# A planned three-layer kernel on one core: the planner's durations set to those of a trace

## Chip, cores, metric

The kernel runs on one core of a Trainium2 chip, as one launch. The metric is device time in microseconds (us) of that launch; lower is better.

## What is computed

Three layers follow one another: local attention, a channel mix with a gate, and a token and channel mixer. Cut to what matters:

```
# attention: 4 batches x 8 heads, 576 positions, head size 64; each position sees 32 others
attn = softmax(mask(q @ k.T / 8)) @ v              # heads 0-3: the last 32; heads 4-7: every 4th of 128
x    = attn, heads side by side                    # (4, 576, 512)
# first mix
x_prev = x moved by one position
xk, xr = mu_k*x + (1-mu_k)*x_prev, mu_r*x + (1-mu_r)*x_prev
x    = sigmoid(xr @ w_r) * (relu(xk @ w_k)**2 @ w_v)      # w_k 512x1024, w_v 1024x512, w_r 512x512
# second mix
u    = x + (relu(x.T @ w_tok1) @ w_tok2).T
out  = u + relu(u @ w_ch1) @ w_ch2
```

The weights arrive as 64-bit floats and are turned into 32-bit ones on the chip.

## The kernel before

**The work.** Attention is cut into 36 units, nine for each batch (`attend`). A unit loads queries and keys (128x832 words, 416 KB) and values (96x512, 192 KB), makes scores on TensorE, a softmax on VectorE and ScalarE, transposes on TensorE, a copy out of PSUM, and then eight small 64x64 matmuls for each transpose group that weigh the values (`weigh`); the result goes to the buffers `xt`. The first nine units run alone; the other 27 are laid beside the first mix. Positions are taken in six chunks of 384. For each chunk `prep` mixes x with its predecessor (`z<-xt,cst`, one step into a scratch buffer, a second that adds), and splits the sum into a high half and a low half, because each fp32 product is made of three fp32r matmuls (`mm3`). `keys` multiplies the key operands with `w_k`, in the order of blocks `KT = [2, 3, 0, 1]` of the 512 channels; `receptance` multiplies with `w_r`; `mix` with `w_v`. For the first chunk the receptance operands are made by TensorE from `x` and diagonal matrices (`bank<-xt,wk`).

**Weights.** `weight` loads a piece into one of two raw buffers, and then takes five steps: ScalarE scales the upper words, VectorE does a shift (`TENSOR_SCALAR`), a bitwise merge and an add in 16-bit halves (two `SCALAR_TENSOR_TENSOR`), a copy gives the high half, and VectorE subtracts for the low half. The next but one piece can be loaded only when VectorE's third step has read the raw buffer. The pieces come in the order: w_k piece 1, w_r pieces 1 to 4, then w_v and w_k in turn.

**What sets the order.** The program is written into `Plan`, which records operations and their dependences. `order` walks a model of time: each engine takes, among the operations that are ready, the one that is due first; a due time is worked out backwards from the order of TensorE's operations in the program, with `_cost` as duration and `DELAY` as time from one engine to another. Copies and a few scalings may go to ScalarE or VectorE (`either`): the plan decides. The order of all five engines is then emitted as one fixed program; each engine keeps its row, in order, and waits on semaphores. All loads are issued by SyncE, in its own planned order. The model also holds a clock of TensorE (`_run`). Line 394 (396 after the change) is the `call(**kw)` that emits every operation, so all instructions carry it; they are told apart by tiles.

Of the kernel before, what the change touches and what calls it, by code (L numbers as in the profile page):

```python
# [64 lines left out]
class View:  # L65


    def __init__(self, slot, kind, array, dtype):
        self.slot, self.kind, self.array, self.dtype = slot, kind, array, dtype
# [76 lines left out]
class Plan:  # L146
# [16 lines left out]
        "sync": dict(tensor=1.09, vector=0.98, scalar=0.98, gpsimd=0.98, sync=1.4),  # L163
    }
    TICK, BUSY = 10.24 / 3, 3060

    def __init__(self, nc):
        self.nc = nc
# [68 lines left out]
    @staticmethod  # L237
    def _cost(engine, method, kw):

        out = kw["out"]  # L240
        cols = int(np.prod(out.shape[1:]))
        if engine == "sync":
            return max(0.45, 4 * cols * out.shape[0] / 310e3)
        if engine == "tensor":
            if method == "transpose":
                return cols / 1200 + 0.0025
            if kw["lhsT"].dtype in (F32R, BF16):
                return cols / 2400 + 0.0135
            if kw["lhsT"].shape[0] <= D or out.shape[0] <= D:
                return cols / 1200 + 0.0025  # L250
            return 2 * max(cols / 1200 + 0.0025, 0.112)
        source = kw.get("in_", kw.get("in0"))
        psum = source is not None and "PSUM" in str(source.space)
        if engine == "scalar":
            extra = sum(hasattr(kw.get(k), "space") for k in ("scale", "bias"))
            extra += 2 * (kw.get("accum_out") is not None)
            return (0.165 if psum else 0.215) + cols / 1200 + 0.093 * extra
        if engine == "gpsimd":
            return 0.04 if method == "memset" else 0.04 + cols / 345
        if method == "tensor_reduce":  # L260
            return 0.145 + int(np.prod(source.shape[1:])) / 960
        if method == "reciprocal":
            return 0.145 + cols / 157
        fast = method in ("tensor_copy", "tensor_scalar", "tensor_scalar_add") and not psum
        return 0.145 + cols / (1920 if fast else 960)

    def _run(self, at, cost, kw):

# [13 lines left out]
    def order(self):  # L282
        n = len(self.ops)
        after = [[] for _ in range(n)]
        for i, deps in enumerate(self.deps):
            for d in deps:
                after[d].append(i)
        first = [next(iter(op)) for op in self.ops]
        cost = [op[e][2] for op, e in zip(self.ops, first)]
        due, t = [1e9 + i for i in range(n)], 0.0  # L290
        for i, e in enumerate(first):
            if e == "tensor":
                due[i], t = t, t + cost[i]
        for i in reversed(range(n)):
            pad = 0 if first[i] == "tensor" else 1.0
            for s in after[i]:
                due[i] = min(due[i], due[s] - cost[i] - self.DELAY[first[i]][first[s]] - pad)
        for i, e in self.early.items():
            due[i] -= e
        for group in self.bursts:  # L300
            due[group[0]] = min(due[i] for i in group)
            for k, i in enumerate(group[1:]):
                due[i] = -1e6 + k
        left = [len(d) for d in self.deps]
        ready = [dict.fromkeys(op, 0.0) for op in self.ops]
        known = {e: [] for e in self.ENGINES}
        avail = {e: [] for e in self.ENGINES}
        free = dict.fromkeys(self.ENGINES, 0.6)
        free["sync"] = 1.7
        start, engine = [None] * n, [None] * n  # L310
        self.tick, self.columns, self.warm, late = 0, 0.0, False, 0.0

        def learn(i):
            for e in self.ops[i]:
                heapq.heappush(known[e], (ready[i][e], i))

        for i in range(n):
            if not left[i]:
                learn(i)
        for _ in range(n):  # L320
            best = None
            for e in self.ENGINES:
                for q in (avail[e], known[e]):
                    while q and start[q[0][1]] is not None:
                        heapq.heappop(q)
                if avail[e]:
                    at = free[e]
                elif known[e]:
                    at = max(free[e], known[e][0][0])
                else:  # L330
                    continue
                if best is None or at < best[0]:
                    best = at, e
            at, e = best
            while known[e] and known[e][0][0] <= at + 0.1:
                _, i = heapq.heappop(known[e])
                if start[i] is None:
                    heapq.heappush(avail[e], (due[i], i))
            aside, chosen = [], None
            while avail[e]:  # L340
                item = heapq.heappop(avail[e])
                i = item[1]
                if start[i] is not None:
                    continue
                ends = {}
                for o in self.ops[i]:
                    ahead = 0.0
                    if o != e:
                        ahead = 1.0 * sum(self.ops[j][o][2] for d, j in avail[o] if d < due[i] and start[j] is None)
                    ends[o] = max(max(at, free[o]) + ahead, ready[i][o]) + self.ops[i][o][2]  # L350
                pick = first[i]
                if ends[pick] > due[i] + cost[i] + late + 0.0:
                    pick = min(ends, key=ends.get)
                if pick == e:
                    chosen = item
                    break
                aside.append(item)
            if chosen is None:
                chosen = aside.pop(0)
            for item in aside:  # L360
                heapq.heappush(avail[e], item)
            i = chosen[1]
            at = max(at, ready[i][e])
            method, kw, length = self.ops[i][e]
            end = at + length
            if e == "tensor":
                end = self._run(at, length, kw)
                late = max(late, at - due[i] if due[i] >= 0 else 0.0)
            start[i], engine[i] = at, e
            free[e] = end  # L370
            for s in after[i]:
                for o in self.ops[s]:
                    ready[s][o] = max(ready[s][o], end + self.DELAY[e][o])
                left[s] -= 1
                if not left[s]:
                    learn(s)
        self.engine = engine
        return sorted(range(n), key=lambda i: (start[i], i))
# [672 lines left out]
```

## Time and profile before

| | |
|---|---|
| runs | 715.89, 716.20, 716.91 us; median 716.2 |
| profiled execution | span 715.3 us from first to last instruction; no time of its own is given beside it. The runs lie 0.6 to 1.6 us above that span |
| TensorE | busy 697.9 us (98%) |
| VectorE, ScalarE | busy 405.1 us (57%), 295.7 us (41%) |
| loads and stores | 53.84 MB, 75 GB/s over the span; about 300 GB/s in the first 30 us |
| TensorE without work | 12.3 us of the first 29.69 us, 1.4 us from there to 56.00 us, none to 711.66 us, 3.6 us at the end |

Since TensorE is busy for 98% of the span, the first 56 us are where its idle time lies.

### The profile page before, as it was taken

What the parts mean: (1) busy time and instruction counts of PE and PEld (TensorE: products, weight loads), DVE (VectorE), ACT (ScalarE), POOL (GpSimd) and SP (SyncE); (2) the same over time, 40 slices, a digit from 0 to 9 for tenths busy, and PEclk for the clock granted to TensorE, in tenths of its full rate; (3) what the DMA queues carried; (4) which work ended last, traced back from release to release, by engine and by line L of the source; (5) the groups of instructions that cost most, each with busy time, mean ns of one, the idle gap of its engine ahead of it and who ended that gap; (6) DMA issues with size and microseconds to landing.
All of it is one profiled execution on the core that took longest, in us unless ns stands there. A gap on an engine that the chain in (4) does not pass through costs nothing.

```text
span 715.3 us, 10559 instructions
## 1 busy us (share of the span) xinstructions
PE 697.9 (98%) x4090; PEld 599.5 (84%) x4090; DVE 405.1 (57%) x915; ACT 295.7 (41%) x825; POOL 2.2 (0%) x22
## 2 busy tenths in 40 slices
PE   6699999999999999999999999999999999999997
PEld 6568988888898888888889988888888888888897
DVE  5799987686586688675888998132123112211121
ACT  5688786565364463453676543121111111111110
POOL 0000000000000000000000000000000000000000
PEclk9799999999999999999999999999999999999999
DMA  8956722224222101103222252001001000100010
GB/s 298 282 203 220 254 76 78 71 89 132 61 71 71 36 9 41 41 15 114 86 74 89 89 175 61 1 0 60 0 1 60 0 1 0 60 1 0 1 60 30
DMA packets 26082, 53.84 MB, mean 75 GB/s; under 512 B 2480, under 2 KB 10032, under 8 KB 26032
## 3 DMA queue, kind: packets, MB, share of 16 engines
q1 hardware_dynamic: 26032, 53.17, 22.9%
q8 instruction: 32, 0.52, 0.3%
q14 instruction: 18, 0.15, 0.1%
HBM read 48.44 MB, written 4.72 MB: 74 GB/s over the span
## 4 chain that ended last, share of the span: by engine, by line
PE 93%; DMA 3%; DVE 1%; ACT 1%; SPq 0%; issue 0%; ACTq 0%
PE bank L394 93%; DMA x<-w_k 1%; DMA wv<-units 1%; DMA x<-w_r 1%; DVE x L394 1%; ACT x L394 1%; SPq L394 0%; DVE z L394 0%; ACT wv L394 0%; ACT z L394 0%; ACT at L394 0%; DVE wr L394 0%; DVE at L394 0%; DVE xt L394 0%; ACTq L394 0%
## 5 line engine op out<-in xcount | busy, mean ns | idle before, releaser
L394 PE MATMUL bank<-z,wk 128*128 128x384 f32 (+2 forms) x816 | 197.7, 357 | 0.5 <-DVE z L394 0.3
L394 DVE SCALAR_TENSOR_TENSOR z<-bank,z 128x512 fp32r<-128x512 f32 (+2 forms) x116 | 70.3, 606 | 218.5 <-ACT z L394 217.7
L394 ACT ACTIVATE z<-bank 128x512 fp32r<-128x512 f32 (+3 forms) x120 | 63.5, 529 | 278.7 <-PE bank L394 277.2
L394 PEld LDWEIGHTS bank<-z,wk 128*128 128x128 f32 x816 | 146.6, 188 | 15.6 <-DVE z L394 0.6
L394 PE MATMUL bank<-wv,z 128*128 128x512 f32 x432 | 125.8, 402 | 0.5 <-ACT wv L394 0.5
L394 PE MATMUL bank<-z,x 128*128 128x512 f32 (+1 forms) x540 | 120.2, 371 | 0.0
L394 PEld LDWEIGHTS bank<-z,x 128*128 128x128 f32 x540 | 94.9, 188 | 18.8
L394 PEld LDWEIGHTS bank<-wv,z 128*128 128x128 f32 x432 | 78.6, 188 | 14.1 <-ACT wv L394 0.6
L394 PE MATMUL bank<-z,at 128*128 128x512 f32 (+1 forms) x276 | 69.0, 383 | 0.0
L394 PE MATMUL bank<-wr,z 128*128 128x512 f32 x228 | 66.8, 404 | 0.0
L394 PEld LDWEIGHTS bank<-z,at 128*128 128x128 f32 x276 | 48.5, 188 | 8.6
L394 DVE TENSOR_TENSOR z<-z,z 128x384 fp32r<-128x384 f32 x92 | 49.9, 551 | 5.6 <-PE bank L394 2.8
L394 PE MATMUL bank<-at 128*128 128x96 f32 (+1 forms) x234 | 40.7, 278 | 11.4 <-DMA at<-cst 5.1
L394 PEld LDWEIGHTS bank<-wr,z 128*128 128x128 f32 x228 | 41.5, 188 | 7.9 <-DVE z L394 0.5
L394 PEld LDWEIGHTS bank<-at 128*128 128x128 f32 x216 | 34.6, 193 | 9.4 <-DMA at<-units 6.3
L394 ACT ACTIVATE x<-bank 96x512 f32<-96x512 f32 (+1 forms) x48 | 28.3, 593 | 32.5 <-PE bank L394 31.9
L394 ACT ACTIVATE z<-z 128x384 fp32r<-128x384 f32 x66 | 33.5, 521 | 13.3 <-PE bank L394 6.8
L394 PE MATMUL bank<-xt,wk 128*128 128x512 f32 (+2 forms) x160 | 38.7, 373 | 0.0
L394 ACT ACTIVATE at<-at 128x96 f32<-128x96 f32 (+2 forms) x104 | 33.8, 327 | 6.2 <-DVE at L394 5.4
L394 PE MATMUL bank<-at,z 128*128 128x288 f32 x192 | 35.5, 303 | 0.0
L394 DVE SCALAR_TENSOR_TENSOR z<-xt,cst,z 128x256 f32<-128x256 f32 (+3 forms) x92 | 33.6, 401 | 0.9 <-ACT z L394 0.7
L394 PEld LDWEIGHTS bank<-at,z 128*128 128x128 f32 x192 | 30.6, 188 | 1.9
(113 smaller groups left out, 789.8 us busy)
## 6 DMA issues: line engine op xcount, KB each, us to landing
at<-units SPq DMA_DIRECT2D x27, 416.0 KB, 3.3
wr<-w_c SPq DMA_DIRECT2D x20, 512.0 KB, 3.6
x<-w_k SPq DMA_DIRECT2D x4, 1024.0 KB, 6.3
x<-w_v SPq DMA_DIRECT2D x4, 1024.0 KB, 5.2
at<-units SPq DMA_DIRECT2D x21, 192.0 KB, 2.6
wv<-units SPq DMA_DIRECT2D x8, 416.0 KB, 6.7
outT<-z SPq DMA_DIRECT2D x9, 256.0 KB, 2.0
x<-w_r SPq DMA_DIRECT2D x4, 512.0 KB, 5.8
```

Of the source, the lines that this page charges most:

```text
L394: call(kw["out"], kw["constant"]) if method == "memset" else call(**kw)
```

## The change

The change edits only numbers in the model of time. The duration of a VectorE or ScalarE operation (the time for which the engine is taken) is cut by about 0.08 to 0.1 us; a new table `TAIL` adds 0.08 (VectorE) and 0.1 us (ScalarE) to the time until a result can be used, so that the time to a result stays nearly as it was. An exponential that also sums costs one read more instead of two. A load's duration becomes eight descriptors' worth of time for each row of its outer dimension in place of bytes over 310 GB/s, and an fp32r matmul's goes from columns/2400 + 0.0135 to columns/2263 + 0.005. No operation is added to the program or taken from it. VectorE gets 932 operations instead of 915, ScalarE 679 instead of 696.

```
+    TAIL = dict(tensor=0.0, vector=0.08, scalar=0.1, gpsimd=0.0, sync=0.0)
...
         if engine == "sync":
-            return max(0.45, 4 * cols * out.shape[0] / 310e3)
+            parts = out.shape[1] if len(out.shape) == 3 else 1
+            return max(0.45, 8 * parts * (0.04 + 4 * cols / parts * 0.0266e-3))
...
             if kw["lhsT"].dtype in (F32R, BF16):
-                return cols / 2400 + 0.0135
+                return cols / 2263 + 0.005
...
-            extra += 2 * (kw.get("accum_out") is not None)
-            return (0.165 if psum else 0.215) + cols / 1200 + 0.093 * extra
+            read = 0.093 * (kw.get("accum_out") is not None)
+            return (0.07 if psum else 0.1) + cols / 1200 + 0.07 * extra + read
...
-            return 0.145 + int(np.prod(source.shape[1:])) / 960
+            return 0.066 + int(np.prod(source.shape[1:])) / 960
...
-        return 0.145 + cols / (1920 if fast else 960)
+        return 0.066 + cols / (1920 if fast else 960)
...
-                due[i] = min(due[i], due[s] - cost[i] - self.DELAY[first[i]][first[s]] - pad)
+                due[i] = min(due[i], due[s] - cost[i] - self.TAIL[first[i]] - self.DELAY[first[i]][first[s]] - pad)
...
-                    ready[s][o] = max(ready[s][o], end + self.DELAY[e][o])
+                    ready[s][o] = max(ready[s][o], end + self.TAIL[e] + self.DELAY[e][o])
```

**SyncE, the first loads of weights.** In the rows below, `x` with `w_k` or `w_r` is a piece of weights, 96x512 are values of a unit, 128x832 its queries and keys; before:

```order
12 L394 DMA wr_0_192<-units 96x512 x2
13 L394 DMA wr_0_209<-units 96x512 x2
14 L394 DMA x_0_226<-w_k 128x4x512
15 L394 DMA wr_0_270<-units 96x512 x2
...
19 L394 DMA at_0_321<-units 128x832 x2
20 L394 DMA at_0_321<-units 96x512
21 L394 DMA x_0_226<-w_r 128x1024
22 L394 DMA at_0_321<-units 96x512 x2
```

and now:

```order
14 L396 DMA wr_0_188<-units 96x512 x2
15 L396 DMA wr_0_211<-units 96x512 x2
16 L396 DMA x_0_232<-w_k 128x4x512
17 L396 DMA wr_0_271<-units 96x512 x2
...
20 L396 DMA at_0_321<-units 128x832 x2
21 L396 DMA at_0_321<-units 96x512 x3
22 L396 DMA x_0_232<-w_r 128x1024
```

Six loads of values (two of them not shown) stand ahead of w_k piece 1 instead of four, and two more than before ahead of w_r piece 2. The first `at<-units 128x832` (unit 9) has the same 23 loads ahead of it in both.

**VectorE, from w_r piece 2 to the key operand of block 0.** `TENSOR_SCALAR x` is the shift of a piece of weights, `z<-xt,cst,z` the second step of a mix (xt_0_71, 73, 75, 77 are the blocks 2, 3, 0, 1 of x), `z<-z,z` a low half; before:

```order
50 L394 TENSOR_SCALAR x_0_226<-x_0_289 128x512
...
58 L394 TENSOR_SCALAR x_0_310<-x_0_328 128x512
59 L394 TENSOR_SCALAR z_0_355<-xt_0_75,cst_0_95 128x384
60 L394 SCALAR_TENSOR_TENSOR x_0_328<-x_0_328,x_0_310 128x512
61 L394 TENSOR_TENSOR z_0_434<-z_0_355,z_0_434 128x384
62 L394 SCALAR_TENSOR_TENSOR x_0_328<-x_0_310,x_0_328 128x512
63 L394 SCALAR_TENSOR_TENSOR z_0_355<-xt_0_75,cst_0_95,z_0_355 128x384
64 L394 TENSOR_SCALAR x_0_226<-x_0_289 128x512
```

and now:

```order
53 L396 TENSOR_SCALAR x_0_232<-x_0_287 128x512
...
59 L396 CAST wr_1_422<-x_0_287 128x512
60 L396 CAST z_0_397<-z_0_352 128x384
61 L396 TENSOR_TENSOR wr_1_422<-x_0_287,wr_1_422 128x512
62 L396 TENSOR_TENSOR z_0_397<-z_0_352,z_0_397 128x384
63 L396 TENSOR_SCALAR x_0_305<-x_0_328 128x512
64 L396 SCALAR_TENSOR_TENSOR x_0_328<-x_0_328,x_0_305 128x512
65 L396 SCALAR_TENSOR_TENSOR z_0_352<-xt_0_77,cst_0_95,z_0_352 128x384
66 L396 COPY xt_0_75<-bank_63 128x192
67 L396 SCALAR_TENSOR_TENSOR x_0_328<-x_0_305,x_0_328 128x512
68 L396 TENSOR_SCALAR x_0_232<-x_0_287 128x512
69 L396 SCALAR_TENSOR_TENSOR z_0_352<-xt_0_75,cst_0_95,z_0_352 128x384
```

The second step for block 0 (`xt_0_75`) moved from 13 to 16 rows behind the shift of w_r piece 2, behind the shift of w_r piece 4; two casts and a copy that ScalarE did before now stand ahead of it (its first step, row 59 before, went to ScalarE in return).

**TensorE, the first keys.** `bank_64<-z,wk` are the matmuls of `keys` for chunk 0 (first z buffer: blocks 2 and 3; second: blocks 0 and 1), `bank_6x<-xt,wk` the diagonal ones; before:

```order
55 L394 MATMUL bank_66<-xt_0_71,wk_0_101 128x384
56 L394 MATMUL bank_63<-x_0_180,z_0_165 64x64 x8
57 L394 MATMUL bank_64<-z_0_434,wk_0_332 128x384 x3
58 L394 MATMUL bank_67<-xt_0_73,wk_0_101 128x384 x2
59 L394 MATMUL bank_64<-z_0_434,wk_0_332 128x384
60 L394 MATMUL bank_68<-xt_0_75,wk_0_101 128x384 x2
61 L394 MATMUL bank_61<-at_0_321 128x96
62 L394 MATMUL bank_64<-z_0_434,wk_0_332 128x384 x2
63 L394 MATMUL bank_64<-z_0_460,wk_0_332 128x384
```

and now:

```order
56 L396 MATMUL bank_63<-x_0_175,z_0_149 64x64 x8
57 L396 MATMUL bank_66<-xt_0_71,wk_0_101 128x384
58 L396 MATMUL bank_64<-z_0_397,wk_0_345 128x384 x6
59 L396 MATMUL bank_64<-z_0_454,wk_0_345 128x384
60 L396 MATMUL bank_67<-xt_0_73,wk_0_101 128x384 x2
61 L396 MATMUL bank_64<-z_0_454,wk_0_345 128x384 x5
62 L396 MATMUL bank_68<-xt_0_75,wk_0_101 128x384 x2
```

The first matmul of block 0 (`z_0_460` before, `z_0_454` now) stood behind four diagonal matmuls and a score; now it stands ahead of them, right behind the six of blocks 2 and 3.

## Rows read from the trace of the kernel before

**Rows 1.** The page, its first line.

```profile
span 715.3 us, 10559 instructions
```

**Rows 2.** Windows by stage: busy time of each engine (instructions), granted clock, DMA share, GB/s.

```profile
0.00:29.69 29.69, 17.37 (x171) 15.34 (x171) 19.32 (x50) 17.24 (x71) 0.69 (x16) 0.93 0.95 303
29.69:56.00 26.31, 24.89 (x179) 19.20 (x179) 24.35 (x46) 21.08 (x58) 0.41 (x4) 0.88 0.61 201
56.00:711.66 655.66, 655.64 (x3741) 564.96 (x3741) 360.95 (x821) 257.37 (x698) 1.06 (x2) 1.00 0.18 60
```

**Rows 3.** Waits of TensorE, whole span: total us, times, longest.

```profile
PE bank L394 <- ACT x L394: 0.6, 3, 0.3
...
PE bank L394 <- ACT wv L394: 0.5, 1, 0.5
...
PE bank L394 <- DVE z L394: 0.3, 1, 0.3
```

**Rows 4.** Timeline of TensorE, 0 to 62 us: start, us, instruction, [idle before].

```profile
29.69 1.59 PE L394 MATMUL bank<-at 128*128 128x96 f32 x6 [4.66 <-DMA at<-units]
...
39.88 0.45 PE L394 MATMUL bank<-z,wk 128*128 128x384 f32 x1
40.65 0.61 PE L394 MATMUL bank<-z,wk 128*128 128x384 f32 x2 [0.32 <-DVE z L394]
...
52.10 2.38 PE L394 MATMUL bank<-z,wk 128*128 128x384 f32 x12 [0.15 <-ACT x L394]
...
56.00 0.73 PE L394 MATMUL bank<-wv,z 128*128 128x512 f32 x2 [0.48 <-ACT wv L394]
```

**Rows 5.** The chain that ended last, in order of time: start, us, what.

```profile
12.06 9.76 DMA x<-w_k
...
26.75 6.94 DMA x<-w_r
```

**Rows 6.** DMA issued from 15 to 30 us.

```profile
DMA packets 2038, 4.53 MB, mean 302 GB/s; under 512 B 215, under 2 KB 215, under 8 KB 2036
...
at<-units SPq DMA_DIRECT2D x3, 192.0 KB, 7.5
```

**Rows 7.** Timeline of ScalarE, 20 to 47 us.

```profile
33.78 0.66 ACT L394 ACTIVATE x<-x 128x512 f32<-128x512 f32 x1 [0.89 <-DMA x<-w_r]
...
42.66 0.53 ACT L394 ACTIVATE z<-z 128x384 fp32r<-128x384 f32 x1
```

**Rows 8.** Timeline of VectorE, 26 to 46 us.

```profile
34.48 0.43 DVE L394 TENSOR_SCALAR x<-x 128x512 uint32<-128x512 uint32 x1 [1.90 <-ACT x L394]
...
35.29 0.68 DVE L394 SCALAR_TENSOR_TENSOR x<-x,x 128x512 uint32<-128x512 uint32 x1
35.89 0.68 DVE L394 TENSOR_TENSOR wr<-x,wr 128x512 fp32r<-128x512 f32 x1
36.49 0.73 DVE L394 SCALAR_TENSOR_TENSOR x<-x,x 128x512 uint16<-128x512 uint32 x1
...
41.15 0.60 DVE L394 SCALAR_TENSOR_TENSOR z<-xt,cst,z 128x384 f32<-128x384 f32 x1
...
43.15 0.55 DVE L394 TENSOR_TENSOR z<-z,z 128x384 fp32r<-128x384 f32 x1
```

**Rows 9.** Groups of VectorE instructions by shape: busy us, mean ns.

```profile
L394 DVE CAST z<-z 128x384 fp32r<-128x384 f32 x26 | 9.3, 358 | 3.2 <-PE bank L394 1.7
...
L394 DVE CAST wr<-x 128x512 fp32r<-128x512 f32 x1 | 0.4, 427 | 0.0
...
L394 DVE COPY xt<-bank 128x192 f32<-128x192 f32 x1 | 0.4, 358 | 0.0
```

**Rows 10.** Windows around the fall of the granted clock, columns as in rows 2.

```profile
22.20:25.60 3.40, 1.01 (x17) 0.64 (x17) 3.06 (x7) 3.20 (x15) 0.00 (x0) 0.99 1.05 287
25.60:29.69 4.09, 0.00 (x0) 0.00 (x0) 2.81 (x5) 1.65 (x8) 0.00 (x0) 0.50 1.04 326
29.69:35.84 6.15, 6.15 (x48) 5.15 (x48) 4.25 (x10) 3.90 (x12) 0.00 (x0) 0.51 0.77 222
```

More of the change, by code (lines that the diff above doesn't have):

```diff
@@ L260, in _cost @@
         if method == "tensor_reduce":
-            return 0.145 + int(np.prod(source.shape[1:])) / 960
+            return 0.066 + int(np.prod(source.shape[1:])) / 960
         if method == "reciprocal":
-            return 0.145 + cols / 157
+            return 0.066 + cols / 157
         fast = method in ("tensor_copy", "tensor_scalar", "tensor_scalar_add") and not psum
-        return 0.145 + cols / (1920 if fast else 960)
+        return 0.066 + cols / (1920 if fast else 960)
     def _run(self, at, cost, kw):
```

## Prediction

> **What bounds the kernel now.** I read the page first: a span of 715.3 us [rows 1]. The windows by stage then say where it can move [rows 2]. From 56.00 to 711.66 us TensorE is busy for 655.64 of 655.66 us, and VectorE, which feeds it, for only 360.95. No order can shorten that stretch, since TensorE's operations stay the same; it could only open gaps in it. From 29.69 to 56.00 TensorE lacks 1.4 us of work, before that 12.3 us. So the time is: when TensorE stops waiting, and what it has done by then.
>
> The first 29.69 us end with a wait of 4.66 us for the queries of unit 9 [rows 4]. The loads run at 302 GB/s there [rows 6], one behind another, and the same 23 loads stand ahead of unit 9 in both orders. TensorE's order puts the same set of work in front of it too. I cost all that is reordered before 29.69 us at nothing: this wait hides it. The list of TensorE's waits and its timeline give what is left behind it: 0.6 us on ScalarE in three pieces, 0.32 on VectorE, 0.48 for w_v [rows 3, 4]. Of these, 0.32, 0.15 and 0.48 (0.95 us together) come after 39.88 us.
>
> **The change, step by step.** It adds no operation; each term is a wait.
>
> *w_r piece 2 comes later.* This load was issued at 26.75 us, when VectorE had freed its buffer, and took 6.94 us, because other loads were in front [rows 5]. The queue's order shows in the chain as well: w_k piece 1 took 9.76 us from issue to landing. Now two more loads of values, 192 KB each [rows 6], stand ahead of both pieces. At 302 GB/s they take 0.4 MB / 302 GB/s = 1.3 us. w_k piece 1 then lands at 21.82 + 1.3 = 23.1, and its five steps end 1.3 us later, which frees the buffer at 28.1; since the queue is full until then, w_r piece 2 lands at 33.70 + 1.3 = 35.0, not later still. Bounds: 0 (transfers overlap and the small ones cost it nothing) to 1.4. I take 1.3, since the queue is the one that made it 6.94 us. ScalarE scaled the piece right after it landed, and VectorE's shift followed at 34.48 [rows 7, 8]; I call the start of this shift D. D becomes 35.8.
>
> *VectorE between D and the operand of block 0.* Behind another instruction, one starts 0.08 us before the one ahead ends: 35.29 + 0.68 is 35.97, the next starts at 35.89 [rows 8]. So the engine is taken for the mean less 0.08. The 16 rows from the shift to the one ahead of the second mix step of block 0 are: three shifts of 0.35, two merges of 0.60, two adds in halves of 0.65, two low halves of w_r of 0.60, two second mix steps of 0.52, two low halves of z of 0.47 [rows 8], and a cast of w_r 0.35, a cast of z 0.28, a copy 0.28 [rows 9]. That is 1.05 + 1.20 + 1.30 + 1.20 + 1.04 + 0.94 + 0.91 = 7.64. The first low half of w_r must wait for ScalarE's copy, which now starts behind the scaling; I add 0.2. The mix step takes 0.60 until its end, the copy of the high half on ScalarE 0.53 [rows 7, 8], and two hand-overs between engines some 0.1 together. The high half of block 0 is ready at D + 7.84 + 0.60 + 0.53 + 0.1 = D + 9.1 = 44.9 us. Before, its mix step started at 41.15, which is D + 6.7 with D = 34.48.
>
> *TensorE ahead of that operand.* Before, TensorE had finished the last 64x64 group and the first diagonal pair at 39.88 us. Now the same set stands ahead of the keys. Four keys of 0.20 us (2.38 us for twelve [rows 4]) bring it to 40.7; the fifth needs the low half that is the tenth of VectorE's rows, ready at D + 5.2 = 41.0 by the same prices (4.97 for ten, 0.2 for the copy). A wait of 0.3, two keys more, and at 41.4 us TensorE stands before the first key of block 0, whose operand is ready at 44.9. **It waits 3.5 us.** Before, four diagonal matmuls and a score lay there. They are queued behind the waiting key now, and so are the receptance operands made from them. If TensorE comes later to this point, the wait shrinks by as much and nothing changes in the end.
>
> *What follows.* From there the work is the same. The weights behind it (w_v piece 1, w_k piece 2) follow VectorE's chain and come 1 to 2 us later, but TensorE is 3 us later too; I let the old waits of 0.95 us go and add none. w_k piece 2 was moved ahead of a unit's load that waits for TensorE; that costs nothing, as VectorE's buffer is the later of its two waits. Sum: 0.3 + 3.5 - 0.95 = 2.85, say 2.9 us. Behind 62 us I cost the new order at nothing: VectorE is taken for little more than half of that stretch [rows 2]. Without this cover each late operand would cost its own delay.
>
> *The clock.* In 22.20 to 25.60 us TensorE was busy for 1.01 us; then the granted clock fell to 0.5 (1.2 GHz), and 6.15 us of work behind the wait ran at 0.51 [rows 10]. That cost half of it, 3.1 us. The new wait is of that kind, 3.5 us with little around it, but work follows at once. Bounds: 0 and 3.1; no row has a gap of this length. It lies between the gap of 4.66 us, at which the clock was down, and those of 0.5 us and less, at which it stayed up; nearer in length to the first, but single. I take 0.8.
>
> The sum is 2.9 + 0.8 = 3.7 us over the profiled span; the runs lie 0.9 us above it in the median, and I carry that along: 716.2 + 3.7 = **719.9 us**.
>
> **A rule of the Trainium skill against a row.** The rows show that a VectorE instruction starts 0.08 us before the one ahead has ended [rows 8]. The Trainium skill, "VectorE: DVE Perf Modes", section "The DRAIN you can't avoid", says that the next op does not start until the pipe is empty, though its next section has exceptions. By that rule the 16 rows would take 16 x 0.08 = 1.3 us more, an estimate, and the wait would be 4.8 us. The trace disagrees, and the row decides.
>
> **Rivals.**
> 1. *The clock falls in the new wait and stays low as long as before.* For it: rows 10. Against it: behind the old drop TensorE stood for 4 us more, here it has work. It gives 716.2 + 2.9 + 3.1 = 722.2. The Trainium skill, "TensorE: Matmul & The Clock Gate", section "What's actually happening", calls the low clock the default that activity releases; by that rule, the trace agrees as far as the fall behind the idle stretch goes.
> 2. *w_r piece 2 is not late.* If the two small loads cost it nothing, D is 34.5 and everything in the chain comes 1.3 to 1.4 us earlier: 716.2 + 1.6 = 717.8 without a fall of the clock, 717.5 if the 0.2 for ScalarE's copy goes too. For it: the load waited longer than its own bytes need. Against it: so did w_k.
> 3. *The wait isn't there, not slower.* The planner takes a ready operation before one that isn't. That it put the key of block 0 ahead of diagonal matmuls that need only x says that, by its account, the operand was ready by then. If its account is nearer than mine, the keys run through, the new waits of 3.8 us are absent, and TensorE's old ones of 0.95 go: 715.3 us, or 714.8 if the other 0.44 behind 29.69 go too. It decides if the operand is ready 2.9 us before my 44.9, at 42.0. For it: VectorE's 1.90 us of idle time before D now hold two operations that came behind it. Against it: 16 instructions on one engine in series, each with a row.
>
> **How the numbers follow.** A change of 0.2% (1.4 us) is about what a measurement of this kernel can tell from none. The forecast, a wait of about 3.5 us with up to half of the old loss of clock, has a chance of 0.60 and runs from 718.3 to 721.5. Rival 1 has 0.15, rival 2 0.14, rival 3 0.09; 0.02 is left for gaps further on. Slower by over 0.2% (above 717.6): 0.60 + 0.15 + 0.07, half of rival 2, = 0.82. Faster (below 714.8): 0.05 of rival 3. Within: the other 0.07 and 0.04, and the 0.02, = 0.13. The range leaves out rival 3 and the end beyond rival 1: 716.8 to 722.3.
>
> **What would show it.** In the changed kernel's profile: w_k piece 1 lands near 23.1 us and w_r piece 2 near 35.0; unit 9's wait still ends near 29.7; a wait of TensorE of 3 to 4 us that ends near 45 us, put down to ScalarE's `z`; from there no idle time; the granted clock low from 25.6 to about 36, perhaps again behind 45. The prediction is wrong if TensorE has no gap over 1 us between 36 and 50 us, if unit 9 lands over 1 us earlier or later, or if gaps appear behind 62 us.

## The result, and the profile after

The changed kernel takes 726.26 us (median of four runs, 723.79 to 727.62), the kernel before 716.56 us (715.89 to 717.23): ratio 1.0128, 95% interval 1.0109 to 1.0148: slower by 1.3%. I had forecast slower, by a wait of 3.5 us ahead of block 0, and 719.9 us in a range up to 722.3. The wait is there, the size is not: 6.4 us are missing.

The profiled execution of the changed kernel took 723.79 us, the fastest of the four; its span is 1.8 us less than its time. First line of its page, and the first row of busy time:

```profile
span 722.0 us, 10557 instructions
...
PE 702.5 (97%) x4090; PEld 602.0 (83%) x4090; DVE 408.2 (57%) x932; ACT 285.8 (40%) x808; POOL 2.5 (0%) x22
```

Windows by stage, to be laid beside [rows 2], and around the two falls of the granted clock, beside [rows 10]:

```profile
0.00:29.69 29.69, 21.02 (x179) 18.58 (x181) 19.51 (x51) 18.07 (x74) 0.69 (x16) 0.94 0.96 306
29.69:56.00 26.31, 21.48 (x156) 16.25 (x157) 24.17 (x46) 17.32 (x42) 0.76 (x4) 0.87 0.55 171
56.00:711.66 655.66, 653.33 (x3703) 560.68 (x3703) 362.22 (x832) 249.95 (x693) 1.04 (x2) 1.00 0.19 61
...
28.02:33.20 5.18, 5.18 (x44) 4.54 (x45) 5.18 (x13) 3.78 (x12) 0.00 (x0) 0.50 0.86 223
...
43.40:46.80 3.40, 3.23 (x6) 2.01 (x7) 3.11 (x6) 0.74 (x2) 0.10 (x1) 0.50 0.91 352
```

The middle stage lacks 4.8 us of TensorE's work instead of 1.4. The long stretch behind 56 us, which had no gap, now lacks 2.3. The second fall of the clock is new: 3.23 us of work at 0.50.

The waits of TensorE (total, times, longest), for [rows 3]:

```profile
PE bank L396 <- ACT z L396: 3.5, 1, 3.5
PE bank L396 <- DVE z L396: 2.0, 2, 1.4
...
PE bank L396 <- ACT x L396: 1.3, 2, 0.8
```

And its timeline, for [rows 4]:

```profile
28.02 1.59 PE L396 MATMUL bank<-at 128*128 128x96 f32 x6 [1.66 <-DMA at<-units]
...
43.56 0.69 PE L396 MATMUL bank<-z,wk 128*128 128x384 f32 x1 [3.55 <-ACT z L396]
...
54.07 1.20 PE L396 MATMUL bank<-at 128*128 128x384 bf16 x9
...
71.17 3.06 PE L396 MATMUL bank<-wr,z 128*128 128x512 f32 x12 [1.40 <-DVE z L396]
...
92.75 1.13 PE L396 MATMUL bank<-z,wk 128*128 128x384 f32 x5 [0.62 <-DVE z L396]
```

The row at 43.56 is the first key of block 0, with the wait that I forecast. Those at 71.17 and 92.75 I had not forecast.

To see where time is lost when the order differs, I take places at which TensorE has done the same number of matmuls of each kind in both kernels, and compare the start of the next instruction in the two traces (after minus before, us; each place is named by what comes next in the kernel before):

```
place (start before)                   changed   changed, second trace
unit 9's scores (29.69)                 -1.67      -0.11
unit 11's scores (50.74)                +3.33      +4.14
a product with w_v piece 1 (64.43)      +2.47      +3.09
a product with w_v piece 3 (95.22)      +5.66      +6.57
end of the span (715.3)                 +6.7       +7.7
```

(The second trace is of a repeat, told below.) Three things stand in it. From unit 9 to unit 11 the order costs 5.0 us (4.2 in the repeat). From 64 to 95 us it costs 3.2 (3.5) more. And behind that another 1.0 to 1.1, in which no wait of TensorE is listed. From unit 9's scores to the end of the span the order costs 8.4 us in all (7.8 in the repeat); the first trace is only 6.7 us longer because its first loads came early.

### The profile page after: what moved, and what is told of

Its sections match the earlier page's. It is cut to its first block, busy times and chain, and to the rows that moved or that the text cites. A ratio compares the mean times of both kernels' runs of the same rounds, so it can differ in the third digit from the quotient of the medians.

```text
span 722.0 us, 10557 instructions
## 1 busy us (share of the span) xinstructions
PE 702.5 (97%) x4090; PEld 602.0 (83%) x4090; DVE 408.2 (57%) x932; ACT 285.8 (40%) x808; POOL 2.5 (0%) x22
## 4 chain that ended last, share of the span: by engine, by line
PE 86%; DVE 4%; DMA 3%; ACT 1%; issue 0%; ACTq 0%
PE bank L396 86%; DMA x<-w_k 2%; DVE x L396 2%; DVE z L396 1%; DMA x<-w_v 1%; ACT x L396 1%; DMA x<-w_r 1%; ACT z L396 0%; DVE at L396 0%; ACT wr L396 0%; ACT xt L396 0%; ACTq L396 0%
## 5 line engine op out<-in xcount | busy, mean ns | idle before, releaser
L396 PE MATMUL bank<-wv,z 128*128 128x512 f32 x432 | 127.5, 402 | 0.0
L396 PE MATMUL bank<-at 128*128 128x96 f32 (+1 forms) x234 | 42.7, 278 | 8.8 <-DMA at<-cst 5.1
L396 PEld LDWEIGHTS bank<-at 128*128 128x128 f32 x216 | 36.3, 193 | 8.7 <-DMA at<-units 4.6
L396 ACT ACTIVATE at<-at 128x96 f32<-128x96 f32 (+2 forms) x115 | 36.1, 317 | 17.8 <-DVE at L396 17.1
L396 ACT ACTIVATE x<-bank 96x512 f32<-96x512 f32 (+1 forms) x45 | 26.6, 593 | 23.0 <-PE bank L396 22.4
L396 PEld LDWEIGHTS bank<-xt,wk 128*128 128x128 f32 x160 | 28.1, 193 | 5.3 <-issue 0.6
```

What stands on the lines that cost most here:

```text
L396: call(kw["out"], kw["constant"]) if method == "memset" else call(**kw)
```

## The experiments

Each was timed against the kernel before on the same chip; diffs are against the changed kernel unless said otherwise. Two questions were open. Which of the new numbers makes the bad order: my theory was the loads' formula, the rival the shorter durations of the engines. And which of the moved operations costs the time: my theory was the late operand of block 0 (w_r piece 2 late, 16 rows on VectorE, TensorE's key ahead of its other work) with the loads of weights behind 50 us, the rivals that the wait only moves on, or that the execution and not the order makes the difference.

### Which of the new numbers does it

**Old durations of loads, new ones of the engines.**

```
-            parts = out.shape[1] if len(out.shape) == 3 else 1
-            return max(0.45, 8 * parts * (0.04 + 4 * cols / parts * 0.0266e-3))
+            return max(0.45, 4 * cols * out.shape[0] / 310e3)
```

> The changed kernel with the duration of a load as it was before; the new durations of VectorE, ScalarE and TensorE stay. In this plan the second mix step of block 0 stands 7 rows behind the shift of w_r piece 2 instead of 16, and all four diagonal matmuls of blocks 3 and 0 stand ahead of the first key of block 0. Theory L (the loads' new duration is too short, and the planner orders for operands that aren't there yet): the wait of 3.55 us is gone, the time is 715 to 719 us. Theory E (the shorter engine durations leave no slack, whatever the loads): 722 us or more, waits of several us behind 30 us.

717.33 us against 716.65, ratio 1.0008 (0.9989 to 1.0026); no wait of TensorE over 0.5 us lies between 30 and 100 us. So the engines' new durations with `TAIL` (TensorE's among them) alone change nothing that can be measured.

**New durations of loads alone, in the kernel before** (the same lines put into it).

> The kernel before with only the duration of a load changed. In this plan the step of block 0 stands 16 rows behind the shift of w_r piece 2, behind the shift of piece 4. Theory L: 721 to 728 us with a wait of 2 us or more between 36 and 50 us. Theory E: 715 to 718 us, as before.

723.45 us, ratio 1.0088 (1.0070 to 1.0105). Its timeline has the wait ahead of the keys too, on VectorE this time, and the clock was at 0.5 behind it, from 48.3 to 51.7 us:

```profile
47.85 2.59 PE L395 MATMUL bank<-z,wk 128*128 128x384 f32 x8 [2.09 <-DVE z L395]
```

The loads' formula does the harm; with the engines' new durations it does some more.

**Half of it.** Old durations for the weights alone, then for the units alone:

```
         if engine == "sync":
+            if out.dtype == U32:
+                return max(0.45, 4 * cols * out.shape[0] / 310e3)
```

> The changed kernel, in which the planner believes the old duration for the loads of the weights alone (bytes over 310e3, 3.38 us for a piece of w_k) and the new one for those of the units. Two theories. Theory H (head): the loads of the units that fill the queue in the first 30 us are believed too short, since they share the queue, so the plan puts the scores of unit 9 and all behind them too early; then this plan loses like the changed kernel, 721 to 726 us, and TensorE waits over 2 us ahead of the weigh of block 0. Theory S (slack): what matters is how early the pieces of the weights, and the shifts behind them, are planned; then this kernel stands at 715.5 to 719 us without a wait over 1 us on z there.

721.88 us, ratio 1.0073 (1.0046 to 1.0101).

```
         if engine == "sync":
+            if out.dtype != U32:
+                return max(0.45, 4 * cols * out.shape[0] / 310e3)
```

> The mirror of the one before: old duration for the loads of the units (1.37 us for scores' and 0.63 us for values' half), new ones for the weights. Theory H: 715.5 to 719 us, no wait over 1 us ahead of block 0. Theory S: 721 to 726 us, and a wait of 2 us or more there. If both kernels lose about half (718.5 to 722 us each), it is the sum of the believed loads ahead of unit 9 that counts, whichever loads they are.

721.68 us, ratio 1.0076 (1.0045 to 1.0107). Each half costs about half of the loss, and both lie in the 718.5 to 722 us that I had set for the case in which the sum of the loads counts, whichever they are; the scaled durations below test that. The waits differ: the first has none over 1.6 us behind 25 us, but 3.4 us of low clock from 38.5; the second keeps the clock and waits for VectorE's `z` for 4.3 us in all.

**Scaled durations.** The new ones times 1.15, and the old ones times 1.15:

```
-            return max(0.45, 8 * parts * (0.04 + 4 * cols / parts * 0.0266e-3))
+            return max(0.45, 1.15 * 8 * parts * (0.04 + 4 * cols / parts * 0.0266e-3))
```

> The changed kernel with the new duration of a load times 1.15, so that the loads up to unit 9 add up to 23.3 us, as the trace of the kernel before has them (23.6 from the landing of unit 0 to that of unit 9), where the change has 20.3. Theory L: 714 to 718 us. Theory E: 722 us or more.

720.78 us, ratio 1.0064 (1.0044 to 1.0084), between the two forecasts, with waits of 3.54 us and 1.96 us at other places than in the changed kernel:

```profile
40.53 0.80 PE L396 MATMUL bank<-z,wk 128*128 128x384 f32 x3 [3.54 <-DVE z L396]
...
68.32 4.61 PE L396 MATMUL bank<-wr,z 128*128 128x512 f32 x12 [1.96 <-DVE z L396]
```

```
-            parts = out.shape[1] if len(out.shape) == 3 else 1
-            return max(0.45, 8 * parts * (0.04 + 4 * cols / parts * 0.0266e-3))
+            return max(0.45, 1.15 * 4 * cols * out.shape[0] / 310e3)
```

> The changed kernel with the old duration of every load times 1.15, so loads are believed longer than the measured mean. If the harm is that loads are believed too short, and a planner that believes them long loses nothing, this stands at 715 to 718 us, no slower than the kernel before. If the old durations were a lucky order, and any other order costs, it stands at 720 us or more.

717.30 us, ratio 1.0009 (0.9996 to 1.0021). So the old durations were not one lucky number: longer ones do as well. But their sum is not all that counts. For the loads from unit 1 to unit 9 the formulas give 20.3 us new and 23.1 old, and 23.3 for the new ones times 1.15, which still loses 0.64%. What differs is the share of each: by the old formula a unit's queries take 1.37 us and a piece of w_r 1.69, by the scaled new one 1.18 and 1.37. Which of these shares matters wasn't tested.

**Old loads and old fp32r duration** (new ones for VectorE and ScalarE alone), to find the loss without a wait behind 100 us:

```
-                return cols / 2263 + 0.005
+                return cols / 2400 + 0.0135
```

> The changed kernel with the old duration of loads and the old duration of an fp32r matmul: new durations for VectorE and ScalarE alone. If the new fp32r duration costs the 1 us between 300 and 400 us, TensorE gains it back there, and the time is 715.5 to 716.5 us, no slower than the kernel before. If the durations of VectorE and ScalarE cost it, the 1 us stays: 716.5 to 718 us.

717.51 us, ratio 1.0007 (0.9996 to 1.0019). Its trace still loses 1.7 us from 300 to 420 us against the kernel before, by the comparison of places; the kernel with old durations of the engines and new ones of loads loses nothing there. So it is not the fp32r number. What in the new order of VectorE and ScalarE does it stays open.

### Which place in the order does it

These keep the changed kernel's plan and move a few operations of its order by hand (`MOVES`: operations, and the one that they now precede).

**The queue: w_k piece 1 and w_r piece 2, each ahead of two loads of values.**

```
+    MOVES = [([319], 138), ([371], 422)]
```

> The plan of the changed kernel as it is, in which two loads alone are moved by hand in the queue: the first piece of w_k ahead of the values of units 4 and 5, and the second piece of w_r ahead of the values of unit 10. My step of the lateness of w_r: the shift of its second piece then starts 4.8 us behind the scores of unit 9, as in the kernel before, and not 6.2 us behind them; the wait ahead of the weigh of block 0 falls from 3.55 to 2.1 us (1.4 less) and the time by 1 to 2 us, to 724 to 725 us. Rival: the second piece of w_r isn't what the chain waits for, the wait stays at 3.2 to 3.6 us and the time within 0.5 us of 726.

724.61 us, ratio 1.0108 (1.0078 to 1.0139). The wait fell by 0.7 us, half of what I expected, as w_r piece 2 landed 4.6 us behind unit 9 instead of 5.5, but ScalarE's scaling of it was behind another operation. From unit 9 to unit 11 this order loses 4.3 us. The time can't be told from that of the changed kernel, whose ratio of 1.0128 lies in this interval.

**VectorE: the second step of block 0 ahead of the shift of w_r piece 3.**

```
+    MOVES = [([296, 297], 380), ([298], 382)]
```

> The changed kernel's plan with three instructions moved by hand: the second mix step of block 0 and the copy of its high half stand ahead of the shift of w_r piece 3, its low half ahead of the third step of piece 3. Nothing else moves. Theory W (the single late operand costs the 3.5 us and the fall of the clock behind it): the wait of 3.55 us shrinks to under 1, the clock does not fall behind 43 us, the time is 720 to 723 us. Rival V (VectorE's total is the limit there, so the wait goes to the next operand): 724 to 728 us, with a wait of 2 us or more at another operand between 38 and 50 us.

726.27 us, ratio 1.0127 (1.0092 to 1.0161): nothing gained. The wait of 3.55 us is gone; in its place there are one on the next block's `z` and one on ScalarE for unit 11's scores:

```profile
47.60 0.61 PE L403 MATMUL bank<-z,wk 128*128 128x384 f32 x2 [1.31 <-DVE z L403]
...
56.58 1.19 PE L403 MATMUL bank<-at 128*128 128x384 bf16 x9 [1.24 <-ACT at L403]
```

and from unit 9 to unit 11 it loses 5.3 us, with a fall of the clock to 0.5 from 40.2 to 43.6 us in it. That fits rival V: one operand was late because of VectorE's whole row of work, and moving that operand forward makes another late, though no single wait reaches the 2 us that I had set for it.

**TensorE: four diagonal matmuls and unit 9's score ahead of block 0's first key again.**

```
+    MOVES = [([307, 308, 311, 312, 349], 332)]
```

> The plan of the changed kernel, in which on TensorE alone the four diagonal matmuls and the score of unit 9 stand ahead of the first key of block 0 again, as in the kernel before. My account says that they fill some 1.7 us of the wait, that the operands made from them come earlier too, and that the wait falls from 3.55 to about 1.8 us; if the granted clock then stays at 1.0 behind it, another 1.7 us is saved: 722.5 to 724.5 us. Rival: VectorE sets the end of the stretch in any case (its rows are the same), and what is saved in this wait returns as waits for its next operands; then the sum of the waits of TensorE from 36 to 60 us stays within 0.7 us and the time at 725.5 to 727.

723.81 us, ratio 1.0092 (1.0066 to 1.0118). The wait shrinks to 0.57 us, a second of 1.08 comes up, and the clock stays up:

```profile
49.04 0.44 PE L403 MATMUL bank<-z,wk 128*128 128x384 f32 x1 [0.57 <-ACT z L403]
50.56 1.14 PE L403 MATMUL bank<-z,wk 128*128 128x384 f32 x5 [1.08 <-DVE z L403]
...
73.18 3.03 PE L403 MATMUL bank<-wr,z 128*128 128x512 f32 x12
```

(This execution is 5.2 us later than the changed kernel's at unit 9.) From unit 9 to unit 11 it loses 3.3 us instead of 5.0. And from 64 to 95 us it loses 1.3 us instead of 3.2 to 3.5: the row at 73.18 is the one that waited for 1.40 us near 71 us, and it waits no more, though no load was moved. Unit 9's score, the last one on unit 9's queries, frees their buffer for those of unit 11. These were issued 17.3 us behind unit 9's first scores here, 21.9 us in the changed kernel (21.2 in the repeat) and 14.6 us in the kernel before; w_k piece 3, further on in the queue, took 5.6 us instead of 7.9.

**The queue behind 50 us: w_v piece 2 ahead of unit 12's queries, w_k piece 3 ahead of unit 13's.**

```
+    MOVES = [([618], 575), ([634], 657)]
```

> The plan of the changed kernel, in which two loads alone are moved in the queue: w_v piece 2 ahead of the queries of unit 12, w_k piece 3 ahead of those of unit 13. Theory (loads of units that wait for TensorE hold up the weights behind 50 us): w_v piece 2 lands 1 to 2 us earlier behind its issue, the waits of 1.40 us near 71 and 0.62 us near 93 shrink to 0.7 us together or less, the early wait of 3.5 us stays, and the time falls by 1 to 2 us to 724 to 725 us. Rival: the pieces are late because VectorE frees the raw buffers late; then both waits stay and the time is within 0.7 us of 726.

728.68 us, ratio 1.0158 (1.0137 to 1.0179): nothing gained, and probably more lost. (This is not the order of the kernel before, which had the queries of both units ahead of both pieces.) The waits near 71 and 93 us go (0.32 is left), but the queue is in order, and unit 12's load now stands behind a piece of weights that waits for VectorE. It lands at 63.8 us instead of 57.3, and TensorE stands for it (SyncE's timeline, then TensorE's):

```profile
56.55 0.37 SPq L403 DMA_DIRECT2D x<-w_v  x1
56.97 0.46 SPq L403 DMA_DIRECT2D at<-units  x1
```

```profile
63.80 1.58 PE L403 MATMUL bank<-at 128*128 128x96 f32 x6 [3.66 <-DMA at<-units]
```

From 64 to 95 us the order loses 1.0 us instead of 3.2, but 4.3 between unit 11's scores and 64 us, where the changed kernel loses nothing.

**The last two moves and that of the first loads together, without and with VectorE's.**

```
+    MOVES = [([319], 138), ([371], 422), ([618], 575), ([634], 657), ([307, 308, 311, 312, 349], 332)]
```

> The moves of the last two and of the run on the queue's order together (six loads or groups of matmuls moved by hand, VectorE and ScalarE as in the changed kernel). If the three losses are separate (loads of w_r, TensorE's order, loads behind 50 us) the savings add up to 3 to 6 us: 720 to 723 us. If VectorE's order alone holds the loss, 724.5 us or more.

```
+    MOVES = [..., ([296, 297], 380), ([298], 382)]
```

> The same, and on VectorE the second mix steps of blocks 0 and the low half behind them moved ahead of the shift of w_r piece 3, as in the run that moved those alone. By my prediction's reading (the operand of block 0 is late, and nothing else) the wait of 3.5 us goes whole: 717 to 720 us. Rival: moving rows on VectorE only changes which operand is late, since VectorE has the same work in the stretch; then not under the run without that move.

727.48 us, ratio 1.0135 (1.0114 to 1.0156), and 727.28, 1.0141 (1.0121 to 1.0162). Both expectations failed on unit 12's load, for which TensorE waits 3.90 and 3.18 us near 62 us. So the 724.5 us or more of the first, set for another reason, says nothing of VectorE. Of the stretch from unit 9 to unit 11 the two still tell something: 2.95 us lost without VectorE's move and 3.46 with it. So the move on VectorE gives nothing here either.

**TensorE's move, and w_k piece 3 alone ahead of unit 13's queries.**

```
+    MOVES = [([634], 657), ([307, 308, 311, 312, 349], 332)]
```

> The changed kernel's plan with TensorE's order at block 0 as before (as in the run that moved that alone) and, of the loads, w_k piece 3 alone ahead of the queries of unit 13; unit 12 stays where it is. If the late unit loads cost the waits near 71 and 93 us: those two are below 0.8 us together, no load of unit 12 is waited for, and the time is 1 to 2 us under the run with TensorE's order alone, 721.5 to 723 us. If w_k piece 3 is late because its buffer comes free late: 723.5 to 725.

721.66 us, ratio 1.0067 (1.0053 to 1.0080). TensorE's timeline around the two places, and SyncE's:

```profile
45.62 0.44 PE L403 MATMUL bank<-z,wk 128*128 128x384 f32 x1 [0.86 <-ACT z L403]
46.94 1.14 PE L403 MATMUL bank<-z,wk 128*128 128x384 f32 x5 [0.88 <-DVE z L403]
...
91.15 1.14 PE L403 MATMUL bank<-z,wk 128*128 128x384 f32 x5 [0.33 <-DVE z L403]
```

```profile
58.54 0.38 SPq L403 DMA_DIRECT2D x<-w_k  x1
59.01 7.94 SPq L403 DMA_DIRECT2D at<-units  x4
```

The load took 5.2 us (landed at 63.7) instead of 7.9; no wait near 71 us is left, and 0.33 near 91. From 64 to 95 us it loses 1.5 us instead of 3.2 to 3.5. Six operations moved, none on VectorE, and 3.7 us of the loss are back. Most of that is TensorE's move, which alone left no wait near 71 us and 1.3 us of loss from 64 to 95. What the load's move adds isn't resolved: counted from unit 9's scores on, the order costs 4.4 us in this trace and 4.8 in that of TensorE's move alone, and the two intervals of the ratio overlap.

**The changed kernel again.** No edit.

> The changed kernel once more. If its loss is the order's, 724 to 728 us again, a ratio of 1.010 to 1.015, with the wait of 3 to 4 us on ScalarE's z ahead of block 0 and one over 1 us near 71 us, whenever unit 9's load lands. If its time is mostly that of the first loads, a trace in which unit 9 lands 1 us later has a span that is about 1 us longer.

725.31 us (724.73 to 727.46), ratio 1.0128 (1.0111 to 1.0144). Its profiled execution is again the fastest of four (span 723.0 us), and shows the same three waits, with other sizes:

```profile
44.38 0.69 PE L396 MATMUL bank<-z,wk 128*128 128x384 f32 x1 [2.84 <-ACT z L396]
...
71.21 3.07 PE L396 MATMUL bank<-wr,z 128*128 128x512 f32 x12 [0.83 <-DVE z L396]
...
93.64 1.14 PE L396 MATMUL bank<-z,wk 128*128 128x384 f32 x5 [1.27 <-DVE z L396]
```

Here unit 9 came 1.56 us later than in the first trace; the first wait is 0.7 us shorter and the span 1.0 us longer. I had expected 3 to 4 us for the wait and over 1 us near 71 us; both are smaller, but the time, the ratio and the cost of the order (7.8 us for 8.4) are about those of before. The sign that I had set for the first loads shows as well (unit 9 later by 1.56 us, the span longer by 1.0), so both add to the time of an execution.

None of these kernels beats the kernel before.

## Why the prediction was wrong

Point by point, by its own steps. Of the three signs that I had set for being wrong, two came: unit 9 landed 1.67 us earlier in the first trace, and gaps appeared behind 62 us.

**"w_r piece 2 comes later": right, measured from unit 9.** D, the start of its shift on VectorE, stood 4.79 us behind unit 9's scores before (34.48 and 29.69). ScalarE's and VectorE's rows of the changed kernel:

```profile
33.54 0.67 ACT L396 ACTIVATE x<-x 128x512 f32<-128x512 f32 x1 [0.37 <-DMA x<-w_r]
...
42.99 0.53 ACT L396 ACTIVATE z<-z 128x384 fp32r<-128x384 f32 x1
```

```profile
34.24 0.43 DVE L396 TENSOR_SCALAR x<-x 128x512 uint32<-128x512 uint32 x1 [0.57 <-ACT x L396]
...
42.07 0.61 DVE L396 SCALAR_TENSOR_TENSOR z<-xt,cst,z 128x384 f32<-128x384 f32 x1
```

D is at 34.24, 6.22 us behind 28.02: 1.4 later, and 0.9 later in the repeat (35.31 and 29.58), where I had 1.3.

**"VectorE between D and the operand of block 0": right.** The 16 rows take from 34.24 to 42.07, 7.83 us for the 7.84 that I summed; ScalarE's copy ends at 43.52, D + 9.3 for D + 9.1. The rule of the Trainium skill that I weighed there ("VectorE: DVE Perf Modes", section "The DRAIN you can't avoid"), taken without the exceptions of its next section, would have had these rows at 9.1 us, by my estimate; the trace disagrees again.

**"It waits 3.5 us": right,** 3.55, and 2.84 where unit 9 came later. The rival in which the wait isn't there fell. The experiment on TensorE shows what the step said in passing, that the matmuls put behind the waiting key are part of the price: ahead of it they take 1.7 us off this stretch (0.9 against the repeat), and the second fall of the clock is gone. What I didn't see is that unit 9's score, put behind the key with them, holds the buffer that the next unit's queries wait for.

**"The clock. I take 0.8": too small.** Behind the wait 3.23 us of work ran at 0.50, which costs 1.6; the repeat has a fall of the same length, from 44.2 to 47.6 us. The old fall gave 0.5 us back, as 5.18 us of work lay in it for 6.15 [rows 10]. So rival 1 was nearer in kind (it does fall), though not in length.

**"What follows ... add none" and "Behind 62 us I cost the new order at nothing": this step failed.** It argued that VectorE is taken for little more than half of the stretch to 711.66 us. That is an average. Windows from 56 to 95 us show VectorE busy for 36 of 39 us, in the kernel before (first row) as in the changed one:

```profile
56.00:95.00 39.00, 39.00 (x298) 34.00 (x299) 36.09 (x67) 31.40 (x97) 0.00 (x0) 1.00 0.63 220
56.00:95.00 39.00, 36.72 (x257) 31.19 (x257) 35.99 (x60) 31.40 (x104) 0.00 (x0) 1.00 0.66 228
```

So VectorE had next to no idle time to cover a late operand, and where I had nothing, the order cost 3.2 us from 64 to 95 us (3.5 in the repeat). Here is the chain that ended last in the changed kernel, in order of time:

```profile
58.07 7.91 DMA x<-w_k
66.00 1.15 ACT x L396
67.17 0.70 DVE x L396
...
72.43 6.29 DMA x<-w_k
...
92.75 213.65 PE bank L396 x1450
```

It runs from load to scaling to shift to load until 92.75 us, and TensorE is not in it. For the wait near 71 us, here are VectorE's rows of the changed kernel, and two of the kernel before:

```profile
67.17 0.70 DVE L396 TENSOR_SCALAR x<-x 128x1024 uint32<-128x1024 uint32 x1 [1.75 <-ACT x L396]
...
68.24 2.44 DVE L396 SCALAR_TENSOR_TENSOR x<-x,x 128x1024 uint32<-128x1024 uint32 x2
70.57 0.55 DVE L396 SCALAR_TENSOR_TENSOR z<-bank,z 128x384 f32<-128x384 f32 x1
```

```profile
64.09 0.55 DVE L394 SCALAR_TENSOR_TENSOR z<-bank,z 128x384 f32<-128x384 f32 x1
64.70 0.70 DVE L394 TENSOR_SCALAR x<-x 128x1024 uint32<-128x1024 uint32 x1
```

In the changed kernel VectorE stands for 1.75 us for w_k piece 3, then does the shift and the merge of that piece and the add of w_v piece 2, and only then the square of the third group of keys (`z<-bank,z`), which frees the bank into which TensorE's next product goes. In the kernel before, this square stood ahead of that shift, so no load could hold it. The piece itself is hardly later than TensorE is: it landed at 65.97 us instead of 63.14, 2.8 us later (as in the repeat), where TensorE was 2.5 us later (3.1 in the repeat). So my argument that TensorE's own lateness covers that of the weights held for the piece; it did not hold for the operation that the new order put behind it, on an engine with no time to spare.

The queue has its part in it. The load of the piece took 7.9 us (7.1 before): the queries of unit 12, which wait for TensorE, landed at 57.3 us instead of 51.3, and those of unit 13, ahead of the piece in both orders, were issued at 55.30 instead of 51.97. With TensorE's move alone, or with that and the piece ahead of unit 13's queries, the load took 5.6 and 5.2 us, VectorE had the piece in time, and the wait near 71 us was gone with VectorE's order unchanged. That the two together, a late load and the square behind it, make this wait follows from the rows; the square alone was not moved back. For the smaller wait near 93 us, again on a square of keys, there are 0.17 us left with TensorE's move alone and 0.33 with both.

**The base.** I laid the sum on a span of 715.3 us and carried 0.9 us from there to the median. Executions of the kernel before that give both are 1.8 us apart, so the profiled one stands for some 717.1 us, above its median, while the profiled one of the changed kernel is 2.5 us below its own. So span against span I had +3.7, and the traces have +6.7. The 3.0 us between them are: -1.7, as unit 9 came earlier; +0.7 up to 50.74 us (5.0 for my 0.3 + 3.5 - 0.32 + 0.8), clock and small waits on ScalarE; -0.2 up to 64 us; +3.2 up to 95; +1.0 behind. The other 3.4 us of the 6.4 lie between executions: 2.5 and 1.8 - 0.9.

**What stays open.** Why the planner with shorter loads makes this order, beyond that either half of the new durations costs about 5 us and 1.15 times the new ones about 4; how much of the 3.2 us from 64 to 95 us is VectorE's order and how much the queue; and the 1 us behind 95 us, most of it between 295 and 405 us.

## What to carry to other kernels

Check a planner's number against the trace in the stretch where it counts. The durations of VectorE and ScalarE were moved towards those of a trace, and nothing measurable changed. The loads' did the harm, and ahead of unit 9 they were not nearer: 20.3 us by the new formula and 23.1 by the old one, where the trace of the kernel before has 23.6 us. Longer durations cost nothing (1.15 times the old ones, 1.0009), but a right sum is not enough (1.15 times the new ones, 23.3 us and 1.0064).

Where a stall is forecast, follow the issue of every load that waits for the stalled engine. The kernel issues its loads in one fixed order, so such a load holds back what stands behind it and shares the transfer time of its neighbours; the run that put unit 12's queries behind a piece that waited for VectorE made TensorE stand for 3.66 us.

A busy share of half over 655 us says nothing about its first 40 us: there VectorE was busy for 36 of 39 us, and what is put behind a load in its row can be late.

## What was not expected of the hardware

**The first loads don't take the same time in each execution.** In the traces whose first 23 loads stand in the order of the changed kernel, unit 9's scores start at 28.02, 28.96, 29.58, 30.25, 30.41 and 33.25 us; in the slowest of these the DMA moved 316 GB/s from 8 to 28 us, in the fastest 341. The spread is as large as what the order costs up to unit 11, and part of it stays in the time: the execution at 33.25 is TensorE's move, which loses 1.7 us less than the changed kernel up to unit 11 and still ends 1.7 us behind that kernel's trace.

**The clock's first rise comes at different times too:** 8.4 us in the trace of before, and 10.1, 12.7 and 15.0 in three traces of the changed kernel's first order. The Trainium skill, "TensorE: Matmul & The Clock Gate", section "What's actually happening", says that the gate's count runs free of the kernel's start, so that such a point moves, by ±500 ns. These traces agree that it moves, but by 4.9 us within one order. Behind waits the clock fell as well, for 3.4 us after 3.55, 2.84 and 3.66 us of idle time, and for 6.8 us after one of 3.14 (the run with w_v piece 2 ahead of unit 12's queries, from 43.4 us). The length of one wait doesn't settle it: in the run of VectorE's move the clock fell from 40.2 to 43.6 us behind waits of 0.65 and 0.77 us, and with the old durations for the units' loads it stayed at 1.0 behind waits of 2.08 and 1.77 us.
